# Dilated window attention and a mixer on one core: batch 1's mask moved to VectorE, with a new order of batch 0's channel mix

## The chip, the cores and the metric

The kernel runs on one core of one Trainium2 chip. The core has TensorE (PE in the views, its weight loads PEld), VectorE (DVE), ScalarE (ACT), GpSimd (POOL) and SyncE (SP), which here only issues DMAs. The metric is the device time of one execution in microseconds; less is better. The time given for a kernel is the median of its runs.

## The reference, cut to what matters

```python
B, H, S, D = 8, 8, 576, 64                      # q, k, v: [B, H, S, D], fp32
scores = q @ k.T / sqrt(D)                      # per batch and head
rel = pos[:, None] - pos[None, :]
mask_plain = (rel >= 0) & (rel < 32)            # heads 0 to 3
mask_dil = (rel >= 0) & (rel < 128) & (rel % 4 == 0)   # heads 4 to 7
attn = softmax(where(mask, scores, -1e9))
x = (attn @ v) -> [B, S, 512]                   # heads side by side
h = relu(x.T @ w_tok1) @ w_tok2                 # token mix: 576 -> 256 -> 576
u = x + h.T
out = u + relu(u @ w_ch1) @ w_ch2               # channel mix: 512 -> 1536 -> 512
```

## The kernel before, in words

All products run in fp16 with fp32 sums in PSUM. The eight batches pass one after the other through the same stages; while the channel mix of batch b runs on TensorE, the attention and the token mix of batch b+1 and the preparation of batch b+2 are woven in between. Tokens are taken in two orders: natural for heads 0 to 3 (the plain ones), by residue modulo 4 for heads 4 to 7 (the dilated ones), so that both masks become narrow bands.

**Attention.** q and k are loaded as fp32 in two halves each, cast to fp16 (`cast_qk`, mostly on GpSimd), and turned. In batches 0 and 1 TensorE turns them (`transposes`, L303), in batch 2 too (`bare_steps`, L363), from batch 3 on a DMA does it from SP's queue (`dma_steps`, L348), and GpSimd puts the keys in natural order (`place_steps`, L393, its copies at L396, L399 and L402). Heads come in four pairs hp, two plain and two dilated. `scores_plain` and `scores_dil` (L453, L479) make the score blocks of batches 0 and 1, in two PSUM banks "sc" used in turn, and ScalarE writes their exponentials to `attp`, `attd` and `attt` (the last for the 64 tail queries). Where `veiled` (L428) holds, a product of the identity with `veil`, a block of 0 and -60000, goes into the bank ahead of each score product (L423) and the exponential of the hidden places becomes 0. Elsewhere the exponentials are multiplied by a band of ones and zeros on GpSimd (`mult` at L112). `values` (L592) multiplies by v with a column of ones, into one of three banks "fl"; VectorE takes the reciprocal of the sum (L616) and multiplies (L617, shown as L112) into `xn`.

**Token mix.** `emit_h1` (L619) and `emit_u` (L630) make u; for batch 0 a special `u_half` (L950) does u in ten halves. `emit_uT` (L656) turns u on TensorE in four column blocks cb, which VectorE or, for cb 2, ScalarE copies to SBUF; from batch 2 on a DMA does it.

**Channel mix.** `gen_main` (L747) makes twelve products gp of 128 hidden channels each (`w3`, four column blocks, 512 columns, L768), with a relu on ScalarE or VectorE into `gta`; then the output yp in four row blocks s (0 to 3), each in two halves of 256 columns over the twelve blocks of `w4` (L801). VectorE adds u (L809) and SP stores (L814). An odd batch also does the tails of two batches (L759, L818). gp and yp share three banks "main".

**The order.** Everything is issued in the order in which the program is written, and every engine works its queue in that order. `interleave` (L827) weaves the steps of `gen_main` with a list of steps that each have a due time and a cost: it keeps a clock t, takes the next step of the list if its due time is not after t, and otherwise the next piece of `gen_main`, whose `yield` is its cost. The times are written out by hand per batch (L1017 to L1053); they set an order, nothing waits for them.

**Queues.** SP issues the loads of q, k and v, the turning DMAs and the stores, in program order. The weights go by GpSimd's queue with a cast: `w3` in three parts (L871), `w4` in three thirds of four blocks each (L998 to L1001), between the casts of batch 1 (`casts1`: tails, then q and k by pairs, then four vn, vt, two vd, vx). A `gate` (L866, a one-element copy on GpSimd) keeps SP's loads of batch 2 behind the first block of `w4` (L1006).

Of the kernel before, what the change touches and what calls it, by code (L numbers as in the profile page):

```python
# [20 lines left out]
DM = 512  # L21
# [47 lines left out]
def kernel(  # L69
# [358 lines left out]
    def veiled(b, hp):  # L428
        return b <= 1
# [23 lines left out]
    def scores_plain(b, hp):  # L453
# [20 lines left out]
        if not veils:  # L474
            mult(nc.gpsimd, blocks[:, :, :, 0:BLK], blocks[:, :, :, 0:BLK], band)
            mult(nc.gpsimd, tail_cols(hp), tail_cols(hp), tails_seen[0])
        yield 0.21

    def scores_dil(b, hp):  # L479
        a = attd[hp - 2]  # L480
        diag = a.rearrange("p h (r c) -> p h r c", c=128)
# [11 lines left out]
        if not veils:  # L493
            mult(nc.gpsimd, diag, diag, band[:, :, :, 0:128])
            mult(nc.gpsimd, tail_cols(hp), tail_cols(hp), tails_seen[1])
        yield 0.12

# [158 lines left out]
    def emit_uT(b, cb):  # L656
        odd = b % 2
        p = bank("fl" if b or cb % 2 == 0 else "main", 3, f"tpu_{b}_{cb}", FP16)
# [87 lines left out]

    def gen_main(b):  # L747
# [17 lines left out]
        for mb in range(NMB):  # L765
            p = bank("main", 3, f"gp_{b}_{mb}")
# [4 lines left out]
            relu(nc.vector if (mb % 2 == 1 and mb < 7 if b == 0 else mb % 4 != 3 if b == 1 else mb in (1, 5)) else nc.scalar, gta[:, mb, m0:m0 + 512], p)  # L771
# [5 lines left out]
        for s in ((4, 0, 1, 2, 3) if odd else (0, 1, 2, 3)):  # L777
# [18 lines left out]
            elif s < 4:  # L796
                for half in range(2):
# [10 lines left out]
                    if half:  # L808
                        nc.vector.tensor_tensor(out=blocks4(o32), in0=blocks4(p), in1=u16(b, s), op=ALU.add)  # L809
                        for i in range(2):  # L810
                            d = slice(256 * i, 256 * i + 256)
                            o = out[b, 0:512, d].rearrange("(m r) c -> r m c", r=4)[s] if i else \
                                out[b, 128 * s:128 * s + 128, d]
                            nc.sync.dma_start(out=o, in_=o32[:, d])  # L814
# [12 lines left out]
    def interleave(main, steps):  # L827
# [3 lines left out]
        while main is not None or steps:  # L831
# [4 lines left out]
            else:  # L836
                try:
                    t += next(main)
# [111 lines left out]
    def u_half(s, half):  # L950
        p = bank("main" if half else "fl", 3, f"up_0_{s}_{half}")[:, 0:256]
# [26 lines left out]
    for s in (1, 2):  # L978
        u_half(s, 1)
    for cb in (1, 2, 3):  # L980
        emit_uT(0, cb)
# [14 lines left out]
    for i in (2, 3, 4, 5, 7, 6, 8, 9, 10, 11):  # L996
        casts1[i]()
    for i in range(3):  # L998
        nc.gpsimd.dma_start(
            out=w4a[:, 4 * i:4 * i + 4],  # L1000
            in_=moe_w_ch2[512 * i:512 * i + 512, :].rearrange("(p i) c -> p i c", i=4))  # L1001
    for cast in casts1[12:]:
# [3 lines left out]
    gate(l32[(2, "t")][0:1, 0, 0:1], w4[0][0:1, 0:1])  # L1006
# [77 lines left out]
```

## Time and profile before

| | |
|---|---|
| median of 3 runs | 287.01 us (286.76 to 287.47) |
| the profiled execution | 286.68 us, span of its instructions 284.8 us |
| granted TensorE clock | 0.999 |
| busy, share of the span | TensorE 276.8 us, 97%; GpSimd 163.5, 57%; ScalarE 136.6, 48%; VectorE 130.3, 46% |
| DMA | 52.63 MB, mean 185 GB/s |

How to read it: a time in the views is counted from the start of the span. TensorE's products are pipelined, so a product is listed as longer than the distance to the next one; what one costs is read from start to start, and a busy share of 97% hides breaks shorter than a product's listed length. A row of the timeline merges like instructions that follow each other (x4 is four of them) and gives the idle time ahead of it with what ended it. In the groups, mean ns is the length of one instruction.

### The profile page before, as it was taken

The page shows a single profiled execution, that of the slowest core. Times are in us where ns is not written, and L with a number is a line of the kernel's source. Part 1 is how long each engine was busy: PE and PEld are TensorE (multiplying, and loading weights), DVE is VectorE, ACT ScalarE, POOL GpSimd, SP SyncE. Part 2 cuts the span into 40 slices and gives each one's busy share as a digit, 9 for nine tenths or more (in the row PEclk, how much of TensorE's full clock was granted, in tenths as well). Part 3 has the DMA queues.
Part 4 walks back from the last instruction along what each step waited for, and adds up shares of the span by engine and source line. Part 5 has one row for each costly group of instructions (what it writes and reads, how often), then busy time and mean ns, then how long its engine had stood idle before and what let it go on. Part 6 is the DMA issues. An engine that isn't in the chain of part 4 may idle for free.

```text
span 284.8 us, 7022 instructions
## 1 busy us (share of the span) xinstructions
PE 276.8 (97%) x2850; PEld 211.3 (74%) x2850; DVE 130.3 (46%) x274; ACT 136.6 (48%) x270; POOL 163.5 (57%) x221
## 2 busy tenths in 40 slices
PE   6999999999999999999999999999999999999995
PEld 2796677887775976697776976797767966886594
DVE  7766757356764155415640254426441274421022
ACT  2873575464454714483446625482546534225500
POOL 7980860479964998459961999079943920000000
PEclk9999999999999999999999999999999999999999
DMA  7999999995999999899889997399784210431023
GB/s 220 265 223 237 278 215 200 319 231 139 334 201 181 272 250 240 108 202 344 214 150 226 315 255 151 57 236 297 196 169 82 94 55 2 95 110 37 0 77 111
DMA packets 105695, 52.63 MB, mean 185 GB/s; under 512 B 73888, under 2 KB 104608, under 8 KB 105664
## 3 DMA queue, kind: packets, MB, share of 16 engines
q1 hardware_dynamic: 101424, 47.07, 67.2%
q0 software_dynamic: 2640, 3.94, 7.9%
q10 hardware_dynamic: 1600, 1.18, 1.4%
q8 instruction: 22, 0.36, 0.5%
q14 instruction: 9, 0.07, 0.1%
HBM read 37.07 MB, written 9.44 MB: 163 GB/s over the span
## 4 chain that ended last, share of the span: by engine, by line
PE 90%; DMA 4%; POOL 2%; ACT 1%; DVE 1%; issue 1%; SPq 0%; POOLq 0%; ACTq 0%
PE yp L801 29%; PE gp L768 28%; PE h1p L627 5%; PE up L639 4%; PE gt L759 4%; PE yp L818 3%; PE sc L510 3%; DMA l_k<-in_k_dram 3%; DMA l_q<-in_q_dram 2%; PE av L603 1%; PE av L608 1%; PE h1p L625 1%; PE sc L425 1%; PE sc L423 1%; PE up L650 1%; PE av L601 1%
## 5 line engine op out<-in xcount | busy, mean ns | idle before, releaser
L801 PE MATMUL yp<-w,gt 128*128 128x256 f16 x744 | 85.8, 273 | 0.0
L801 PEld LDWEIGHTS <-gt 128*128 128x128 f16 x744 | 76.1, 106 | 6.4
L106 ACT ACTIVATE gt<-gp 128x512 f16<-128x512 f32 x72 | 43.0, 597 | 75.4 <-PE gp L768 75.1
L768 PE MATMUL gp<-utd,w 128*128 128x512 f16 x144 | 54.7, 380 | 0.0
L768 PE MATMUL gp<-utm,w 128*128 128x512 f16 x144 | 54.6, 379 | 0.0
L768 PEld LDWEIGHTS <-w 128*128 128x128 f16 x384 | 39.0, 114 | 19.9 <-issue 0.5
L809 DVE TENSOR_TENSOR o<-yp,u 128x512 f32<-128x512 f32 x31 | 21.4, 691 | 63.1 <-PE yp L801 54.7
L112 POOL TENSOR_TENSOR attp<-attp,const 128x1280 f16<-128x1280 f16 x12 | 31.4, 2615 | 26.6 <-ACT attp L534 26.5
L112 DVE TENSOR_TENSOR xn<-av,rec 128x320 f16<-128x320 f32 x64 | 31.4, 491 | 2.2
L112 POOL TENSOR_TENSOR attd<-attd,const 128x1024 f16<-128x1024 f16 x12 | 25.4, 2138 | 0.7 <-ACT attd L534 0.7
L768 PE MATMUL gp<-uT,w 128*128 128x512 f16 x96 | 25.6, 379 | 0.0
L108 DVE TENSOR_SCALAR gt<-gp 128x512 f16<-128x512 f32 x24 | 16.5, 687 | 12.0 <-PE gp L768 11.5
L645 DVE TENSOR_TENSOR u<-up,xn 128x512 f16<-128x512 f32 x26 | 17.9, 690 | 6.2 <-PE up L639 6.2
L534 ACT ACTIVATE attp<-sc 128x480 f16<-128x480 f32 (+1 forms) x36 | 16.1, 539 | 7.2 <-PE sc L510 7.2
L102 POOL CAST c_k<-l_k 128x512 f16<-128x512 f32 x29 | 17.8, 622 | 2.0 <-DMA l_k<-in_k_dram 2.0
L102 POOL CAST c_q<-l_q 128x512 f16<-128x512 f32 x27 | 17.4, 650 | 2.5 <-DMA l_q<-in_q_dram 2.5
L616 DVE RECIPROCAL rec<-av 128x5 f32<-128x5 f32 x64 | 12.2, 191 | 13.5 <-PE av L613 13.3
L106 ACT ACTIVATE h<-h1p 128x256 f16<-128x256 f32 x31 | 11.9, 383 | 12.1 <-PE h1p L627 11.7
L399 POOL COPY kt<-kr 128x512 f16<-128x512 f16 x10 | 10.8, 1079 | 10.0 <-DMA kr<-c_k 4.6
L697 ACT COPY utd<-utm 128x512 f16<-128x512 f16 x12 | 12.7, 1130 | 4.0 <-DMA utm<-u 4.0
L102 POOL CAST vv<-l_vn 128x256 f16<-128x256 f32 x32 | 11.8, 412 | 3.8 <-DMA l_vn<-in_v_dram 3.8
L112 POOL TENSOR_TENSOR attt<-attt,const 128x512 f16<-128x512 f16 x12 | 13.9, 1162 | 0.0
(149 smaller groups left out, 465.3 us busy)
## 6 DMA issues: line engine op xcount, KB each, us to landing
out_dram<-o SPq DMA_DIRECT2D x71, 128.0 KB, 3.2
l_q<-in_q_dram SPq DMA_DIRECT2D x15, 512.0 KB, 6.7
l_k<-in_k_dram SPq DMA_DIRECT2D x14, 512.0 KB, 7.0
l_vn<-in_v_dram SPq DMA_DIRECT2D x32, 128.0 KB, 6.5
l_vd<-in_v_dram SPq DMA_DIRECT2D x16, 256.0 KB, 4.6
w<-in_moe_w_ch_dram POOLq DMA_DIRECT2D x6, 512.0 KB, 8.1
lt<-in_q_dram SPq DMA_DIRECT2D x8, 128.0 KB, 5.0
l_vt<-in_v_dram SPq DMA_DIRECT2D x8, 128.0 KB, 4.7
```

The lines of the kernel that those rows point to most:

```text
L102: eng.tensor_copy(out=out, in_=in_)
L106: nc.scalar.activation(out=out, in_=in_, func=AF.Relu)
L108: eng.tensor_scalar_max(out=out, in0=in_, scalar1=0.0)
L112: eng.tensor_tensor(out=out, in0=x, in1=y, op=ALU.mult)
L534: nc.scalar.activation(out=out, in_=in_, func=AF.Exp, scale=0.125)
L616: nc.vector.reciprocal(out=rec[:, :, 0], in_=av[:, :, 64])
L627: nc.tensor.matmul(out=p, lhsT=w[:, s, j], rhs=x[:, s, c], start=False, stop=(s == 3))
L645: nc.vector.tensor_tensor(out=u16(b, s), in0=blocks4(p), in1=blocks4(xn[b][:, s]), op=ALU.add)
L697: nc.scalar.copy(out=natural(uTd[:, cb - 2]), in_=uTm[i][:, cb].rearrange("p r m -> p m r"))
L768: nc.tensor.matmul(out=p, lhsT=w3_block(cb, mb), rhs=uT[(b, cb)][0], start=(i == 0), stop=(i == 3))
L801: nc.tensor.matmul(out=p[:, c], lhsT=gta[:, mb, a0:m0 + 512:4] if half else gta[:, mb, a0:a0 + 128], rhs=w4[mb][:, c], start=(mb == 0), st ...
L809: nc.vector.tensor_tensor(out=blocks4(o32), in0=blocks4(p), in1=u16(b, s), op=ALU.add)
```

## The change

Four edits, with the times of the list moved to suit.

1. **Batch 1 masked by VectorE.** `veiled` holds for batch 0 alone. Batch 1's scores have no product with the veil; a new `mask_pair` multiplies one pair's exponentials and its tails by the band, and the list of batch 0 calls it on VectorE for all four pairs, ahead of the values. Batch 1's cast of q for pair 1 goes from GpSimd to ScalarE.
2. **Batch 0's output by thirds.** Row blocks 0 to 2 of batch 0's output are summed in three rounds, over blocks 0 to 3, 4 to 7 and 8 to 11 of `w4`, with all three banks "main" held. A piece of `gen_main` may now yield ("from", time), which puts the planner's clock forward to 19.2 and 22.4. The first third of `w4` is issued by GpSimd ahead of three of batch 1's v casts, the other two behind them; the gate of batch 2's loads waits for the second third.
3. **Channel product begun amid u.** For the first three gp of batch 0 the column blocks 0 and 1 are multiplied (`gp_first`) between the last u halves and the transposes of column blocks 2 and 3; `gen_main` adds 2 and 3. Two transposes and one u half change their banks for it, and the relus of gp 5 and 6 are on VectorE.
4. **Batch 3's transposes ahead of v.** In batch 1's list the loads of v and the turning DMAs of batch 3 are mixed: four v loads, tails and first k, three v loads, first q and second k, the last v load, second q. GpSimd's placing of keys moves ahead of the last v casts.

```diff
     def veiled(b, hp):
-        return b <= 1
+        return b == 0
...
+    def mask_pair(hp, eng):
+        if hp < 2:
+            w = plain_blocks(hp)[:, :, :, 0:BLK]
+            mult(eng, w, w, band)
+        else:
+            w = attd[hp - 2].rearrange("p h (r c) -> p h r c", c=128)
+            mult(eng, w, w, band[:, :, :, 0:128])
+        mult(eng, tail_cols(hp), tail_cols(hp), tails_seen[hp // 2])
...
+    def gp_first(mb, cb):
+
+        if mb == len(first):
+            first.append(bank("main", 3, f"gp_0_{mb}"))
+        nc.tensor.matmul(out=first[mb], lhsT=w3[0][:, cb, mb:512:4], rhs=uT[(0, cb)][0],
+                         start=(cb == 0), stop=(cb == 3))
...
         for mb in range(NMB):
+            if b == 0 and mb < 3:
+                gp_first(mb, 2)
+                gp_first(mb, 3)
+                relu(nc.vector if mb == 1 else nc.scalar, gta[:, mb, 0:512], first[mb])
+                yield 0.43
+                continue
...
+        if b == 0:
+            ps3 = [bank("main", 3, f"yp_{b}_{s}") for s in range(3)]
+            for i in range(3):
+                if i:
+                    yield ("from", (0.0, 19.2, 22.4)[i])
+                for s, p in enumerate(ps3):
+                    for half in range(2):
+                        c = slice(256 * half, 256 * half + 256)
+                        for mb in range(4 * i, 4 * i + 4):
+                            nc.tensor.matmul(
...
+                        if half or i < 2:
+                            yield 0.43
+                    if i == 2:
...
+                        store(s, o32)
+                        yield 0.43
-        for s in ((4, 0, 1, 2, 3) if odd else (0, 1, 2, 3)):
+        for s in ((4, 0, 1, 2, 3) if odd else (0, 1, 2, 3) if b else (3,)):
...
-                    t += next(main)
+                    d = next(main)
+                    t = max(t, d[1]) if isinstance(d, tuple) else t + d
...
     emit_uT(0, 0)
-    for s in (1, 2):
-        u_half(s, 1)
-    for cb in (1, 2, 3):
-        emit_uT(0, cb)
+    u_half(1, 1)
+    emit_uT(0, 1)
+    gp_first(0, 0)
+    u_half(2, 1)
+    gp_first(1, 0)
+    gp_first(2, 0)
+    for mb in range(3):
+        gp_first(mb, 1)
+    emit_uT(0, 2)
+    emit_uT(0, 3)
...
-    for i in (2, 3, 4, 5, 7, 6, 8, 9, 10, 11):
+    for i in (2, 4, 5, 7, 6, 8):
         casts1[i]()
...
+    load_w4(0)
+    for i in (9, 10, 11):
+        casts1[i]()
+    load_w4(1)
+    load_w4(2)
     for cast in casts1[12:]:
         cast()
 
     new_qk(2)
-    gate(l32[(2, "t")][0:1, 0, 0:1], w4[0][0:1, 0:1])
+    gate(l32[(2, "t")][0:1, 0, 0:1], w4[4][0:1, 0:1])
...
         if b == 0:
+            steps += at(2.9, 0.0, [lambda: cast_qk(1, "q", 1, nc.scalar)])
             steps += score_steps(1, 0, 0, (0.0, 0.7, 1.5),
-                                 ((3.0, 5.2), (4.4, 7.0), (7.2, 9.6), (8.6, 11.4)))
-            va = value_steps(1, 13.4, 0.7)
-            steps += va[:4] + [(p + 0.3, c, f) for p, c, f in va[4:]]
-            steps += mix_steps(1, 18.4, 20.8, 22.8, 31.4, 1.1)
-            steps += at(24.0, 0.3, cast_steps(2))
+                                 ((3.0, 4.9), (4.3, 6.6), (6.9, 9.2), (8.3, 11.0)))
+            steps += at(12.2, 0.0, [lambda: mask_pair(0, nc.vector), lambda: mask_pair(1, nc.vector)])
+            steps += at(13.0, 0.0, [lambda: mask_pair(2, nc.vector)]) + at(13.4, 0.0, [lambda: mask_pair(3, nc.vector)])
+            steps += value_steps(1, 15.0, 0.75)
+            steps += mix_steps(1, 19.5, 22.3, 24.4, 30.0, 1.0)
+            steps += at(23.8, 0.3, cast_steps(2))
...
-            scores2 = score_steps(2, 29.6, 4.4, lag=0.25)
+            scores2 = score_steps(2, 31.4, 4.4, lag=0.25)
...
         elif b == 1:
...
-            steps += at(6.0, 0.0, [lambda: load_v(3)]) + at(20.8, 0.9, load_steps(4))
-            steps += at(11.0, 0.9, dma_steps(3)) + at(16.4, 0.4, place_steps(3))
+            steps += at(20.8, 0.9, load_steps(4))
...
+            steps += at(6.0, 0.0, [lambda: some_v(0, 4)]) + at(8.1, 0.0, [turns[0], turns[2], lambda: some_v(4, 7)])
+            steps += at(10.6, 0.0, [turns[1], turns[4], lambda: some_v(7, 8)]) + at(12.6, 0.0, [turns[3]])
+            steps += at(11.0, 0.3, casts[9:14]) + at(12.5, 0.0, places[0:3])
+            steps += at(13.0, 0.3, casts[14:16]) + at(14.0, 0.0, places[3:]) + at(14.2, 0.0, casts[16:])
```

More of the change, by code (lines that the diff above doesn't have):

```diff
@@ L809, in gen_main @@
                         nc.vector.tensor_tensor(out=blocks4(o32), in0=blocks4(p), in1=u16(b, s), op=ALU.add)
[L810 to L814, printed above, removed]
+                        store(s, o32)
                     yield 0.65
```

38 lines of the change are left out of this document (24 added, 14 removed).

## The prediction

> **What bounds the kernel now.** I read the chain that ended last first, then TensorE's timeline from the end of batch 0's u to the end of batch 1's channel product (20 to 95 us), then GpSimd's, VectorE's and the SP queue's over the same stretch.
>
> ```profile
> PE 90%; DMA 4%; POOL 2%; ACT 1%; DVE 1%; issue 1%; SPq 0%; POOLq 0%; ACTq 0%
> ...
> 79.30 1.73 PE gp L768 x8
> ...
> 95.04 7.97 PE yp L801 x72
> ```
>
> The first line is the chain by engine: TensorE has 90% of it. The two pieces give its pitch: 1.73/8 = 0.216 us for a channel product of 512 columns, 7.97/72 = 0.111 us for an output product of 256. Time therefore goes where TensorE gets less work or fewer breaks; an operation on another engine counts only where TensorE waits for it. The change edits the stage from 26 to 67 us (batch 0's channel mix, with batch 1's attention woven in) and one wait at 89 us. Later batches have the same code.
>
> **Veils taken off TensorE: -2.4 us.** Every score product of batch 1 has an identity product of the same shape ahead of it (L423), whose start to the next start is its price:
>
> ```profile
> 34.95 0.19 PE L423 MATMUL sm<-veil,const 128*128 128x64 f16 x1
> 34.98 0.19 PE L425 MATMUL sm<-qz,kt 128*128 128x64 f16 x1
> ...
> 35.18 0.23 PE L423 MATMUL sc<-veil,const 128*128 128x160 f16 x1
> 35.25 0.23 PE L425 MATMUL sc<-qz,kt 128*128 128x160 f16 x1
> ...
> 37.94 0.22 PE L423 MATMUL sc<-veil,const 128*128 128x128 f16 x1
> 38.00 0.22 PE L425 MATMUL sc<-qz,kt 128*128 128x128 f16 x1
> ```
>
> That is 0.03, 0.07 and 0.055 us. From the code, two plain pairs have 6 products of 160 columns, 2 of 128 and 4 of 64 each; two dilated pairs have 8 of 128 and 4 of 64. So 12 x 0.07 + 20 x 0.055 + 16 x 0.03 = 2.4 us, all of it on TensorE and in the chain.
>
> **Channel product begun amid u: +0.26 us.** Six of batch 0's products (three rows of blocks by two column blocks) are issued before the transposes of column blocks 2 and 3 instead of behind them.
>
> ```profile
> 26.02 0.91 PE L673 MATMUL tpu<-const,u 128*128 128x128 f16 x8
> ...
> 27.38 0.11 PEld L768 LDWEIGHTS <-w 128*128 128x128 f16 x1 [0.28 <-issue]
> 27.71 2.05 PEld L768 LDWEIGHTS <-w 128*128 128x128 f16 x10 [0.22 <-issue]
> ```
> ```profile
> 26.74 0.58 ACT L100 COPY uT<-tpu 128x512 f16<-128x512 f16 x1 [0.38 <-PE tpu L673]
> ...
> 26.97 0.69 DVE L102 COPY uT<-tpu 128x512 f16<-128x512 f16 x1 [0.33 <-PE tpu L673]
> ```
>
> Now the third product waits for ScalarE's copy (to 27.32) and the fourth for VectorE's (to 27.66); the fourth starts at 27.71, so the eighth at 27.71 + 4 x 0.216 = 28.57. After the change the six products fill the breaks around the last u, and the eight transposes come behind them: six products of 0.216 more in front, less the breaks they fill, move the end of the transposes from 26.7 to 27.8. Behind them stands nothing that needs no copy. Reading the trace's distances (last transpose of a block to the end of its copy 0.9 to 1.0 us), the seventh product starts at about 28.5 and the eighth at 28.83. The breaks are moved, not removed: 0.26 us later. Bounds: -0.4 if the copies overlap better, +0.5 if the six products also wait for PSUM banks of u.
>
> **Breaks among the scores: 0, within 0.8.** The pieces up to the first output product:
>
> ```profile
> 42.01 0.19 PE L603 MATMUL av<-vv,attp 128*128 128x65 f16 x1
> ...
> 42.29 0.60 PE L768 MATMUL gp<-uT,w 128*128 128x512 f16 x2
> ...
> 46.51 0.28 PE L608 MATMUL av<-vv,attd 128*128 128x65 f16 x4
> ...
> 46.70 0.27 PE L625 MATMUL h1p<-xn,w1t 128*128 128x256 f16 x1
> ...
> 47.24 0.29 PE L608 MATMUL av<-vv,attd 128*128 128x65 f16 x4
> ...
> 48.83 0.82 PE L801 MATMUL yp<-w,gt 128*128 128x256 f16 x6
> ```
>
> A plain head's value products take 0.28 us, a dilated head's 0.19, one h1 product 0.54. From 28.57 to 48.83 are 20.26 us; less veils (2.4), eight heads (4 x 0.28 + 4 x 0.19 = 1.9) and two h1 products (1.1), which the change moves behind the first output products, 14.9 remain. Work in that is 41 channel products (8.84), 36 transposes (36 x 0.055 = 2.0) and the scores (2.4, as the veils), 13.2 us: 1.7 us are breaks, for casts, for VectorE's copies of keys and for the two score banks that ScalarE has to empty. After the change the scores follow each other in half the time, so the banks turn more slowly beside them; but a half of a channel product stands between more of them. Laying out the new order I find four breaks of 0.1 to 0.6 us, again 1.7. The first output product then starts at 28.83 + 13.2 + 1.7 = 43.7.
>
> **Weight thirds: 0.** GpSimd issues the first third of w4 before three of batch 1's v casts, and one q cast goes to ScalarE.
>
> ```profile
> 29.91 0.77 POOL L871 DMA_DIRECT2D w<-in_moe_w_ch_dram  x1
> ...
> 33.86 1.17 POOL L102 CAST c_k<-l_k 128x512 f16<-128x512 f32 x2 [0.16 <-DMA l_k<-in_k_dram]
> ...
> 38.51 1.61 POOL L999 DMA_DIRECT2D w<-in_moe_w_ch_dram  x3
> 40.10 0.43 POOL L102 CAST vv<-l_vn 128x256 f16<-128x256 f32 x1
> 40.44 0.64 POOL L102 CAST vv<-l_vt 64x512 f16<-64x512 f32 x1
> 41.00 1.20 POOL L102 CAST vv<-l_vd 128x512 f16<-128x512 f32 x2
> 42.29 0.40 POOL L102 CAST vt<-l_vx 128x256 f16<-128x256 f32 x1
> 44.50 0.18 POOL L867 CAST lt<-w 1x1 f32<-1x1 f16 x1 [1.81 <-DMA w<-in_moe_w_ch_dram]
> ```
> ```profile
> DMA to landing us min/median/max: 5.1/7.9/10.6
> ```
>
> The last k cast ends at 35.0, so the third leaves then and lands at 42.9 by the median for w: 0.8 before 43.7. It costs nothing, down to 0.8 later; at the slowest landing, 45.6, TensorE waits 1.9. w3's last part (issued 29.91, so 37.8) is needed by the ninth row of products at about 38.3, 0.5 later. The second and third thirds are wanted only at about 50. What is queued behind: the v casts, wanted by the values at 45, and the gate of batch 2's loads, which now waits for the second third. It opens at 44.50 now and about 1 to 2 us later then. Batch 2's transposes and scores are also put later, by about as much in their places, so I count 0.
>
> **Masks on VectorE, and the values behind them: +0.9 us.** VectorE gets four masks and four tail masks, and queued behind them on VectorE are the reciprocals and products of all eight heads, for whose PSUM banks TensorE waits. The trace shows no product of two SBUF operands on VectorE; the nearest rows:
>
> ```profile
> L112 DVE TENSOR_TENSOR xn<-av,rec 128x320 f16<-128x320 f32 x64 | 31.4, 491 | 2.2
> ...
> L809 DVE TENSOR_TENSOR o<-yp,u 128x512 f32<-128x512 f32 x31 | 21.4, 691 | 63.1 <-PE yp L801 54.7
> ```
> ```profile
> 55.11 0.28 DVE L372 COPY kt<-tp_t 128x256 f16<-128x256 f16 x1
> ...
> 65.23 0.42 DVE L387 COPY kr<-tp_k 128x512 f16<-128x512 f16 x1 [0.22 <-PE tp_k L378]
> ```
> ```profile
> 45.25 0.18 DVE L616 RECIPROCAL rec<-av 128x5 f32<-128x5 f32 x1
> ...
> 45.88 0.18 DVE L616 RECIPROCAL rec<-av 128x5 f32<-128x5 f32 x1
> ```
>
> Products with an fp32 operand grow by (691 - 491)/192 = 1.04 ns an element, dense fp16 copies by 0.14/256 = 0.55 ns. The masks are dense fp16 (1280, 1280, 1024, 1024 elements and four of 256). By the products' line they take 2 x 1.49 + 2 x 1.22 + 4 x 0.42 = 7.1 us, by the copies' line 2 x 0.84 + 2 x 0.70 + 4 x 0.28 = 4.2. I take 4.2, since operands, type and stride are those of the copies, and keep 7.1 for the range. In the layout above the last key transposes of batch 1 start at 39.0 and VectorE's copy of them ends at about 40.4, so the masks end at 44.6; three half-thirds of output (0.44 each) put the first head on TensorE at 45.0 and its reciprocal at 45.5. So the masks are hidden with 0.9 to spare; at 7.1 they would end at 47.5, 2.0 too late, and the whole gain below would be gone. The Trainium skill gives the reason in "VectorE: DVE Perf Modes", section on the perf-mode tier table: a tensor_tensor on 16-bit SBUF operands runs at two elements a cycle, one with fp32 or PSUM at one. By that rule the masks take 4.2 and the sum stays; the two lines above, fp32 against fp16, agree with it, though neither has both operands in SBUF.
>
> Not hidden is what follows. One head takes VectorE 0.63 us (45.25 to 45.88), 0.66 with the plain ones. Five heads and two h1 products now stand together on TensorE with three banks between them. The second h1 product needs the bank of the seventh head: 45.5 + 7 x 0.66 = 50.1. TensorE's own work from 45.0 up to there (eight heads 1.9, three half-thirds 1.3, one h1 0.54) would let it start at 48.7: breaks of 1.5, rounded. In the trace these heads hid under channel products. From 48.83 to the stage's end at 67.44 are 18.6 us; the same count of pieces (96 output products, two h1, u, 56 transposes, batch 2's first scores) leaves about 0.6 of breaks there, mostly before batch 2's transposes, which now come later than their data. So 1.5 - 0.6 = +0.9, between -0.6 (neither) and +1.5 (both).
>
> **Batch 3's transposes ahead of v: -0.6 us.**
>
> ```profile
> 67.44 1.03 PE L768 MATMUL gp<-uT,w 128*128 128x512 f16 x4
> ...
> 88.58 0.38 PE L510 MATMUL sc<-qt,kt 64*128 64x160 f16 x6
> 89.31 0.44 PE L510 MATMUL sc<-qt,kt 64*128 64x160 f16 x8 [0.35 <-POOL kt L399]
> ```
> ```profile
> 83.39 1.28 SPq L351 DMA_TRANSPOSE kr<-c_k  x1
> ```
> ```profile
> 88.19 1.06 POOL L399 COPY kt<-kr 128x512 f16<-128x512 f16 x1
> ```
>
> The keys of batch 3 are turned by a DMA that SP issues at 83.39, behind all eight v loads; GpSimd then places them to 89.25, and TensorE has stood since about 88.8. The change puts tails and first keys ahead of four v loads, so about 5 us sooner. These transposes wait for GpSimd's casts, and behind them on SP now wait those v loads and the second half of q; the v casts come later for it, but batch 3's values are a stage away. The break of 0.5 and the tenth before it go. If TensorE comes to this place 1.2 us sooner (2.4 - 0.26 - 0.9), the unmoved order would have cost as much more, so the move also keeps what the rest wins.
>
> **Sum.** -2.4 + 0.26 + 0 + 0 + 0.9 - 0.6 = -1.8 us. The profiled execution took 286.68 us (span 284.8, 1.9 around it); so 284.9 against it. The median of the three runs is 287.01, 0.33 above it: 285.2 us.
>
> **The rivals.**
>
> *Masks meet GpSimd's casts.* Between 40 and 45 us GpSimd casts v: 0.43 + 0.64 + 1.20 + 0.40 = 2.7 us. If each operation that starts first holds up the other, up to 2.7 us falls on the masks; they end at 47.3, 1.8 later than the first reciprocal, and all banks with it. Of the gain of 1.8 nothing is left: 287.0. Against it: casts come as v lands, in pieces, and half of them may fall on GpSimd instead. The Trainium skill states this lock in "SBUF — State Buffer", section on who interferes with whom: a VectorE operation with two SBUF inputs and a GpSimd one that reads SBUF exclude each other. No operation of that kind is in the trace of before, so it neither agrees nor differs. Chance 0.13.
>
> *VectorE becomes the bound (slower).* The masks run by the products' line, 7.1 us, and half of the casts (1.35) fall on them: end at 40.4 + 8.45 = 48.9, 3.4 past the first reciprocal. Against the gain of 1.8 that is +1.6: 288.6. It decides once the masks end later than 45.5 + 1.8 = 47.3. For it: the only products in the trace run at that line. Against: both have an fp32 operand in them. Chance 0.11.
>
> *Loads take the win.* Either w4's first third lands as late as the slowest w (1.9 us of TensorE's time), or the gate opens 2 us later and batch 2's masks on GpSimd come late for its values: a gain of 0 to 0.4, about 286.8. This is the case of a change that doesn't bring its weight sooner. For it: DMA engines are full in this stretch. Chance 0.09.
>
> *No new breaks.* TensorE runs on through the values (-1.5) and the lead-in costs nothing (-0.3): 283.4. Chance 0.15.
>
> **How the numbers follow.** Forecast 285.2, chance 0.52; its own range by the bounds of breaks and lead-in is 284.1 to 286.4. About 0.3% (0.9 us) is what a measurement of this kernel can tell from no change: below 286.1 is faster, above 287.9 slower. Faster: forecast and the last rival and a little of the others, 0.66. Same: 0.22. Slower: 0.12. The range leaves out the slower rival and what lies beyond the last one: 283.2 to 287.2.
>
> **What would show it.** Right: no L423 after 20 us; mask rows of about 0.84 and 0.70 us on VectorE; TensorE's breaks between the first head and the second h1 product about 1.5 us, released by VectorE; batch 1's first channel product at about 66.2 instead of 67.44; no wait for L399 at batch 3's first scores. Wrong: mask rows over 1.2 us or starting only when GpSimd's casts end; TensorE standing for w before the first output product; values of batch 2 waiting for GpSimd's masks; a break among the scores over 1 us.

## The result and the profile after

The changed kernel takes 292.00 us (median of 6 runs, 289.70 to 293.01) against 286.88 us for the kernel before in the same session (6 runs, 286.17 to 287.56): 1.0167 times as long, interval 1.0137 to 1.0197. It is slower by 1.7%, where I forecast 285.2. The profiled execution took 292.29 us, its span 290.4. The six executions differ in the granted clock: one at 1.000 took 289.70 us, two at 0.993 and 0.994 took 291.71 and 290.76, three at 0.987 and 0.988 took 292.29 to 293.01; the profile is one of these three.

The page of the changed kernel, the line of 40 slices with the granted clock and the chain by engine:

```profile
PEclk9999999797999999999999999999999999999999
...
PE 83%; DMA 6%; SPq 3%; issue 2%; DVE 2%; POOL 2%; ACT 1%; POOLq 0%; ACTq 0%
```

TensorE had 90% of the chain before, DMA 4%, "issue" 1% and SP's queue nothing; now TensorE has 83%, and DMA, SP's queue and "issue" together 11%. And two slices, near 50 and near 70 us, show a lower granted clock, which the kernel before did not have there. Next, TensorE's timeline of the changed kernel from 30 us on, with only the rows that show a wait, then the first product of batch 1's channel mix and batch 3's first scores:

```profile
34.29 0.38 PE L425 MATMUL sc<-qz,kt 128*128 128x160 f16 x3 [0.45 <-DVE kt L314]
...
36.56 0.38 PE L425 MATMUL sc<-qz,kt 128*128 128x160 f16 x3 [0.36 <-DVE kt L314]
...
41.29 0.38 PE L425 MATMUL sc<-qz,kt 128*128 128x128 f16 x4 [0.40 <-ACT attd L484]
...
49.27 0.19 PE L613 MATMUL av<-vt,attt 128*128 128x65 f16 x1 [1.26 <-POOL vt L102]
...
50.40 0.27 PE L627 MATMUL h1p<-xn,w1t 128*128 128x256 f16 x1 [0.54 <-DVE rec L618]
...
51.58 0.37 PE L627 MATMUL h1p<-xn,w1t 128*128 128x256 f16 x1 [0.17 <-ACT h L106]
...
65.06 0.80 PE L512 MATMUL sc<-qt,kt 64*128 64x160 f16 x12 [0.28 <-ACT uT L100]
...
66.28 0.23 PE L512 MATMUL sc<-qt,kt 64*128 64x128 f16 x2 [0.42 <-DVE uT L102]
...
68.06 0.59 PE L675 MATMUL tpu<-const,u 128*128 128x128 f16 x4 [1.38 <-ACT attt L536]
...
73.78 1.03 PE L785 MATMUL gp<-uT,w 128*128 128x512 f16 x4
...
94.91 0.65 PE L512 MATMUL sc<-qt,kt 64*128 64x160 f16 x14
```

The stage ends at 73.78 where it ended at 67.44: 6.3 us lost between 26 and 74 us. From there to the end of the span are 216.6 us, against 217.4 before: 0.7 comes back, at the row at 94.91, batch 3's first scores, which no longer wait for GpSimd. The idle time in brackets is counted from a product's listed end; from start to start, less what the product before it costs, the breaks are 0.15 to 0.2 longer (1.42 at 49.27, 1.54 at 68.06).

Why TensorE waits at 49.27 is read from the queues. SP's issues of the last v load and of batch 2's first load in the kernel before:

```profile
34.75 1.50 SPq L207 DMA_DIRECT2D l_vx<-in_v_dram  x1
44.70 0.61 SPq L196 DMA_DIRECT2D lt<-in_q_dram  x1
```

The same two in the changed kernel:

```profile
34.49 1.60 SPq L207 DMA_DIRECT2D l_vx<-in_v_dram  x1
49.37 0.61 SPq L196 DMA_DIRECT2D lt<-in_q_dram  x1
```

And GpSimd's timeline in the changed kernel:

```profile
34.66 0.54 POOL L1048 DMA_DIRECT2D w<-in_moe_w_ch_dram  x1
...
38.23 1.07 POOL L1048 DMA_DIRECT2D w<-in_moe_w_ch_dram  x2
...
42.65 1.06 POOL L102 CAST vv<-l_vd 128x512 f16<-128x512 f32 x1 [1.84 <-DMA l_vd<-in_v_dram]
48.82 0.40 POOL L102 CAST vt<-l_vx 128x256 f16<-128x256 f32 x1 [5.11 <-DMA l_vx<-in_v_dram]
49.16 0.18 POOL L909 CAST lt<-w 1x1 f32<-1x1 f16 x1
```

The last v load of batch 1 (l_vx) leaves SP a quarter of a microsecond sooner than before, and yet lands at 48.8; before, its cast began at 42.29. That is 14.3 us from issue to landing instead of 7.5, with all three thirds of the output weight under way beside it. GpSimd stands 5.1 us for it, and the gate, which is behind that cast in GpSimd's queue, opens at 49.16 instead of 44.50. So batch 2's loads are 4.7 us late as well (whether that costs anything is the second experiment's question).

The clock, by windows of 2 us (busy time of PE, PEld, DVE, ACT and POOL, then granted clock, DMA share, GB/s):

```profile
48.00:50.00 2.00, 0.60 (x15) 0.46 (x13) 1.05 (x4) 0.00 (x0) 0.52 (x2) 1.00 0.06 13
50.00:52.00 2.00, 1.43 (x14) 1.07 (x15) 1.90 (x7) 0.38 (x1) 0.00 (x0) 0.76 0.41 93
52.00:54.00 2.00, 2.00 (x11) 1.40 (x10) 0.17 (x1) 0.38 (x1) 0.61 (x1) 0.50 0.88 242
54.00:56.00 2.00, 2.00 (x18) 1.73 (x17) 0.00 (x0) 0.38 (x1) 0.61 (x1) 0.89 1.10 367
...
68.00:70.00 2.00, 1.94 (x15) 1.69 (x15) 1.21 (x2) 1.86 (x5) 0.98 (x1) 0.52 0.67 134
70.00:72.00 2.00, 2.00 (x17) 1.66 (x16) 0.01 (x1) 0.58 (x1) 2.00 (x2) 0.62 0.89 292
```

The DMA engines are nearly idle from 48 to 50 us (share 0.06): everything waits for the gate. And behind each group of breaks TensorE gets half its clock for a while. The clock missing from 50 to 56 us is 2 x (0.24 + 0.50 + 0.11) = 1.7 us, that from 68 to 72 is 2 x (0.48 + 0.38) = 1.7 us: two stretches of 3.4 us at 0.50. A row listed as busy 2.00 there does half the work: twelve output products take 2.2 us from 52.60 on, where they took 1.3 from 44.01 on.

Last, the masks on VectorE, four of eight rows:

```profile
40.53 0.95 DVE L112 TENSOR_TENSOR attp<-attp,const 128x1280 f16<-128x1280 f16 x1
...
42.55 0.68 DVE L112 TENSOR_TENSOR attd<-attd,const 128x1024 f16<-128x1024 f16 x1
43.15 0.70 DVE L112 TENSOR_TENSOR attt<-attt,const 128x256 f16<-128x256 f16 x1
...
44.38 0.28 DVE L112 TENSOR_TENSOR attt<-attt,const 128x256 f16<-128x256 f16 x1
```

They end at 44.66 and are hidden. A meeting with GpSimd shows: its cast at 42.65 begins just behind the mask at 42.55 and takes 1.06 instead of 0.63 us; the mask at 43.15 begins while that cast runs and takes 0.70 instead of 0.28. By the Trainium skill ("SBUF — State Buffer", on who interferes with whom) the later of two such operations is blocked until the earlier one is done; the trace agrees, at 0.4 us each time.

### The profile page after: what moved, and what is told of

Read it like the earlier page. It is cut to its first block, busy times and chain, and to the rows that moved or that the text cites. A ratio compares the mean times of both kernels' runs of the same rounds, so it can differ in the third digit from the quotient of the medians.

```text
span 290.4 us, 6934 instructions
## 1 busy us (share of the span) xinstructions
PE 277.5 (96%) x2802; PEld 210.9 (73%) x2802; DVE 134.7 (46%) x283; ACT 136.1 (47%) x270; POOL 163.4 (56%) x220
## 4 chain that ended last, share of the span: by engine, by line
PE 83%; DMA 6%; SPq 3%; issue 2%; DVE 2%; POOL 2%; ACT 1%; POOLq 0%; ACTq 0%
PE yp L846 26%; PE gp L785 25%; PE h1p L629 5%; PE up L641 4%; PE gt L770 4%; PE yp L859 4%; DMA l_vd<-in_v_dram 3%; PE sc L512 3%; SPq L207 2%; PE yp L811 2%; DMA w1p<-in_moe_w_tok_dram 2%; DMA l_q<-in_q_dram 1%; PE h1p L627 1%; PE av L610 1%; PE av L605 1%
## 5 line engine op out<-in xcount | busy, mean ns | idle before, releaser
L846 PE MATMUL yp<-w,gt 128*128 128x256 f16 x672 | 77.3, 275 | 0.0
L106 ACT ACTIVATE gt<-gp 128x512 f16<-128x512 f32 x71 | 42.4, 597 | 71.6 <-PE gp L785 70.3
L846 PEld LDWEIGHTS <-gt 128*128 128x128 f16 x672 | 69.5, 107 | 5.9
L785 PEld LDWEIGHTS <-w 128*128 128x128 f16 x372 | 38.0, 114 | 19.4
L854 DVE TENSOR_TENSOR o<-yp,u 128x512 f32<-128x512 f32 x28 | 19.4, 692 | 59.6 <-PE yp L846 55.8
L112 DVE TENSOR_TENSOR xn<-av,rec 128x320 f16<-128x320 f32 x64 | 31.5, 492 | 2.2
L108 DVE TENSOR_SCALAR gt<-gp 128x512 f16<-128x512 f32 x25 | 17.2, 688 | 12.2 <-PE gp L785 10.7
L785 PE MATMUL gp<-uT,w 128*128 128x512 f16 x84 | 22.0, 380 | 0.0
L102 POOL CAST c_q<-l_q 128x512 f16<-128x512 f32 x26 | 16.8, 653 | 3.1 <-DMA l_q<-in_q_dram 3.1
L656 DVE TENSOR_TENSOR u16t<-up,xn 64x512 f16<-64x512 f32 x7 | 4.8, 688 | 20.7 <-PE up L652 20.7
```

The lines of the kernel that those rows point to most:

```text
L102: eng.tensor_copy(out=out, in_=in_)
L106: nc.scalar.activation(out=out, in_=in_, func=AF.Relu)
L108: eng.tensor_scalar_max(out=out, in0=in_, scalar1=0.0)
L112: eng.tensor_tensor(out=out, in0=x, in1=y, op=ALU.mult)
L785: nc.tensor.matmul(out=p, lhsT=w3_block(cb, mb), rhs=uT[(b, cb)][0], start=(i == 0), stop=(i == 3))
L846: nc.tensor.matmul(out=p[:, c], lhsT=gta[:, mb, a0:m0 + 512:4] if half else gta[:, mb, a0:a0 + 128], rhs=w4[mb][:, c], start=(mb == 0), st ...
```

## The experiments

The theory after the result: the weight, issued sooner, takes the DMA engines from the last v load; that makes TensorE wait and opens the gate late (the wait is shown below, a cost of the late gate is not); batch 2's transposes and scores then meet the transposes of batch 1's u in the three banks "fl"; and each group of breaks brings half clock. The rivals: the gate's new condition is to blame, or the new order of products has lost its cover whatever the loads do. All ratios are against the kernel before, run beside each on the same chip: 286.61 us for the first four kernels, 286.73 for edits 1, 3 and 4 alone and the mended kernel, 286.53 for the loads alone and the last two.

**The gate on the first third (changed kernel).**

```diff
-    gate(l32[(2, "t")][0:1, 0, 0:1], w4[4][0:1, 0:1])
+    gate(l32[(2, "t")][0:1, 0, 0:1], w4[0][0:1, 0:1])
```

> The changed kernel, with the gate of batch 2's loads back on the first third of w4. Theory A (the gate's one-element copy stands in GpSimd's queue behind the last v cast, whose load landed at 48.8 us, so the tile that it names decides nothing): the gate opens at 49.2 as in the changed kernel, time unchanged within 0.3%. Rival B (waiting for the second third makes batch 2 late): the gate opens about 44.5 and the time falls by 1 to 2 us.

Measured: 291.34 us, 1.0128 [1.0080, 1.0177], which can't be told from the changed kernel's 1.0167. GpSimd's gate copy still starts at 49.53, because it stands behind the cast of l_vx, which waits to 49.19. The condition of the gate is not what holds it; its place in the queue is.

**The second and third third of the weight behind the v casts (and the gate on the first).**

```diff
-    load_w4(1)
-    load_w4(2)
     for cast in casts1[12:]:
         cast()
+    load_w4(1)
+    load_w4(2)
```

> The changed kernel, with the second and third thirds of w4 issued behind all v casts of batch 1, and the gate on the first third. Theory A (those thirds crowd out the last two v loads): the last v load lands near 43.5 instead of 48.8, TensorE's break of 1.4 us before the fifth head is gone, the half clock from 51 to 54.5 us (1.7 us) too, the gate opens near 44.5 and batch 2's data come some 3 to 4 us sooner: 2.5 to 4 us less than the changed kernel (288 to 289.5). Rival (the first third alone crowds the v load out, or the later thirds come too late for the second round of the output): break of over 1 us stays, time within 0.5% of the changed kernel.

Measured: 290.13 us, 1.0105 [1.0072, 1.0137]. GpSimd in this kernel:

```profile
43.82 0.46 POOL L102 CAST vt<-l_vx 128x256 f16<-128x256 f32 x1
44.22 1.12 POOL L1048 DMA_DIRECT2D w<-in_moe_w_ch_dram  x2
45.33 0.18 POOL L909 CAST lt<-w 1x1 f32<-1x1 f16 x1
```

The cast no longer waits, so the load was in by 43.8, five microseconds sooner (8.9 us after its issue, against 14.3), and the gate opens at 45.33. The break for vt is gone; those that are left before the second h1 product are 0.53, 0.53 and 0.45 us, all released by VectorE and ScalarE. So the two late thirds did starve the v load, and repairing that brings back 1.6 of the 5.1 us, less than the 2.5 to 4 expected: three of the four executions still ran at 0.993 or 0.994.

The breaks at batch 2 are the same to 0.01 us, with 1.54 at the worst. But the open gate did not bring batch 2's data sooner, as the two thirds now stand beside these loads. GpSimd's first cast of batch 2 in the changed kernel:

```profile
53.38 0.61 POOL L102 CAST c_t<-lt 128x512 f16<-128x512 f32 x1 [4.04 <-DMA lt<-in_k_dram]
```

And with the thirds behind the v casts:

```profile
54.90 0.62 POOL L102 CAST c_t<-lt 128x512 f16<-128x512 f32 x1 [9.39 <-PE up L652]
```

The first is the load of the k tails, which takes 3.2 us from issue to landing in the changed kernel and 8.6 in this one. Its data come 1.5 us later and the breaks are the same: so the late gate of the changed kernel is not what makes them.

**The last two transposes of batch 1's u in the other banks (changed kernel).**

```diff
-        p = bank("fl", 3, f"tpu_{b}_{cb}", FP16) if b or cb % 2 == 0 else bank("sc", 2, f"tpu_{b}_{cb}", FP16)
+        p = bank("main", 3, f"tpu_{b}_{cb}", FP16) if b == 1 and cb % 2 else \
+            bank("fl", 3, f"tpu_{b}_{cb}", FP16) if b or cb % 2 == 0 else bank("sc", 2, f"tpu_{b}_{cb}", FP16)
```

> The changed kernel, with the last two transposes of batch 1's u in banks main instead of fl. Theory C (they stand right behind batch 2's first scores, which hold the three fl banks until ScalarE has done four small exponentials): the break of 1.5 us before them falls under 0.4, and the half clock from 68 to 71.5 (1.7 us) goes with it: 1.5 to 3 us less than the changed kernel, 289 to 290.5. Rival (the wait is for the late data of batch 2 and only moves): under 0.8 us less.

Measured: 290.33 us (288.44 to 291.38), 1.0103 [1.0071, 1.0135]. TensorE's rows that answer, these transposes, the output products behind them and the next wait:

```profile
64.79 0.40 PE L675 MATMUL tpu<-const,u 128*128 128x128 f16 x4
...
65.67 0.82 PE L846 MATMUL yp<-w,gt 128*128 128x256 f16 x6
...
68.39 0.38 PE L378 MATMUL tp_k<-const,c_k 128*128 128x128 f16 x4 [0.58 <-DVE kt L388]
```

The break of 1.54 before the transposes is 0.09 now: the banks were its cause. But the output products behind them now wait 0.31, and a new break of 0.75 comes at 68.39 for VectorE's copy of keys, so only 0.4 us of it is gained. The stage ends at 69.9 in this execution, which is one of full clock. This kernel also prices the half clock: its eight executions fall into three at a granted clock of 1.000 (288.44 to 288.71 us) and five at 0.994 (290.24 to 291.38). The same instructions, with medians 1.9 us apart. A stretch of 1.7 us lost in 290 is 0.006 of the clock, so 0.994 is one such stretch and the 0.987 of the changed kernel's profile is two.

**Idle products in the two worst breaks (changed kernel).** Six products of 512 columns without use at due time 17.5 and six at 31.5; they add work to the kernel and take nothing out.

```diff
+    def fill(tag, bufs, n):
+        p = bank(tag, bufs, f"fill_{tag}")
+        for _ in range(n):
+            nc.tensor.matmul(out=p, lhsT=idle[:, 0:128], rhs=idle, start=True, stop=True)
...
+            steps += at(17.5, 0.0, [lambda: fill("sc", 2, 6)]) + at(31.5, 0.0, [lambda: fill("main", 3, 6)])
```

> The changed kernel, with six idle products of 512 columns (1.3 us) on TensorE ahead of the fifth head of batch 1 and six ahead of the last two transposes of u, each in the place of a wait of about 1.5 us. They compute nothing that is used. Theory D (the granted clock falls to a half for some 3.4 us after such a wait, which costs 1.7 us each time): clock 1.00 through both stretches, 2 to 3.4 us less than the changed kernel, 288.6 to 290. Rival (the half clock has another cause): clock as in the changed kernel, time the same or up to 0.5 us more.

Measured: 289.55 us (289.29 to 290.29), 1.0093 [1.0064, 1.0123]; against the 291.34 of the gate's kernel beside it, which has the breaks open. The windows:

```profile
50.00:52.00 2.00, 1.32 (x15) 1.07 (x16) 1.90 (x7) 0.38 (x1) 0.00 (x0) 1.00 0.53 116
52.00:54.00 2.00, 2.00 (x21) 1.84 (x20) 0.14 (x1) 0.39 (x1) 0.56 (x1) 1.00 0.94 260
...
68.00:70.00 2.00, 2.00 (x29) 1.92 (x27) 1.00 (x4) 1.47 (x4) 2.00 (x1) 1.00 0.63 149
```

The late v load, the late gate and the other breaks are still there; only the two waits are filled and the half clock is gone, in all four executions, and with it 1.8 us. The time is that of the changed kernel's one execution at full clock, 289.70. So the half clock follows from TensorE's standing and is a cost of its own.

**Edit 1 alone on the kernel before, without its q cast: masks on VectorE, values later.**

```diff
-        return b <= 1
+        return b == 0
...
+            steps += at(12.2, 0.0, [lambda: mask_pair(0, nc.vector), lambda: mask_pair(1, nc.vector)])
+            steps += at(13.0, 0.0, [lambda: mask_pair(2, nc.vector)]) + at(13.4, 0.0, [lambda: mask_pair(3, nc.vector)])
+            steps += value_steps(1, 16.0, 0.7)
+            steps += mix_steps(1, 20.6, 22.6, 24.2, 31.4, 1.1)
```

> The kernel before with the masks of batch 1 on VectorE and its values later, and nothing else of the change: the weight of the output product is issued and landed as before. Theory (TensorE saves the veils' 2.4 us, but arrives at the first output product at about 43.4 us, where the weight lands by parts at 44.4, 46.8 and 50.2 in the kernel before): TensorE waits 2 to 4 us in all for the weight instead, so the time is 286.5 to 288.5. Rival (the order of products fills the gap, and nothing else is short): the whole 2.4 us less, 284.5. The rival is also what my forecast would have said of this part alone.

Measured: 292.65 us, 1.0197 [1.0167, 1.0228]: slower, and by more than I expected. TensorE's waits:

```profile
44.90 0.61 PE L804 MATMUL yp<-w,gt 128*128 128x256 f16 x4 [1.26 <-DMA w<-in_moe_w_ch_dram]
...
47.35 1.01 PE L804 MATMUL yp<-w,gt 128*128 128x256 f16 x4 [1.84 <-DMA w<-in_moe_w_ch_dram]
...
50.52 1.01 PE L804 MATMUL yp<-w,gt 128*128 128x256 f16 x4 [2.16 <-DMA w<-in_moe_w_ch_dram]
```

From start to start, less the product before it, 1.43, 2.01 and 2.37: 5.8 us, with half clock from 46.58 to 53.41. Without the veils, and with values and h1 moved behind, TensorE is at the output product at 43.5 us, where it came at 48.8 before, and the weight lands when it always did. My theory had the right wait and missed its size, as I had left out that all twelve blocks are needed by the first half, and the clock.

**The loads of edit 2 alone on the kernel before.** Nothing else: veils, whole output products and all times of the list as before, but for the one q cast on ScalarE.

```diff
-    for i in (2, 3, 4, 5, 7, 6, 8, 9, 10, 11):
+    for i in (2, 4, 5, 7, 6, 8):
         casts1[i]()
...
+    load_w4(0)
+    for i in (9, 10, 11):
+        casts1[i]()
+    load_w4(1)
+    load_w4(2)
...
-    gate(l32[(2, "t")][0:1, 0, 0:1], w4[0][0:1, 0:1])
+    gate(l32[(2, "t")][0:1, 0, 0:1], w4[4][0:1, 0:1])
```

> The kernel before with only the loads of the change: the weight's first third issued ahead of three casts, the second and third right behind them, the gate hung on the second third, one q cast on ScalarE; the veils, the whole output products and all else as before. Theory (the late v load and the late gate cost by themselves): the last v load of batch 1 lands at about 48 us instead of 42.2, its first reader on TensorE (45 to 46.6 us before) waits 2 to 3 us for it, and batch 2's first transposes wait 1 to 2 us at 57 us; with the half clock that follows, 289.5 to 292. Rival (the loads were harmless, and the loss of the change belongs to the products that now come without cover): 286.5 to 287.5.

Measured: 293.93 us, 1.0245 [1.0218, 1.0272], the slowest of all. GpSimd's row for vt in this kernel:

```profile
49.32 0.40 POOL L102 CAST vt<-l_vx 128x256 f16<-128x256 f32 x1 [4.27 <-DMA l_vx<-in_v_dram]
```

TensorE's row behind it:

```profile
49.77 0.21 PE L611 MATMUL av<-vt,attt 128*128 128x65 f16 x1 [5.39 <-POOL vt L102]
```

That is one wait of 5.6 us from start to start, less the product before it. The windows of this kernel at that place:

```profile
46.00:48.00 2.00, 0.00 (x0) 0.00 (x0) 0.00 (x0) 0.00 (x0) 0.00 (x0) 0.77 0.49 95
48.00:50.00 2.00, 0.23 (x3) 0.21 (x3) 0.00 (x0) 0.00 (x0) 0.52 (x2) 0.50 0.05 10
50.00:52.00 2.00, 2.00 (x12) 0.91 (x10) 1.37 (x4) 0.60 (x1) 0.00 (x0) 0.50 0.28 65
52.00:54.00 2.00, 2.00 (x14) 1.20 (x13) 0.67 (x2) 0.60 (x1) 0.00 (x0) 0.53 0.82 191
```

The place and the cause are the theory's; the wait is twice what I gave it, since it is the fifth head that reads vt and it was ready at 44.2. The other wait of the theory did not come: the gate opens at 49.66, and yet TensorE has no break over 0.1 us from 49.8 to 64 us, so the late gate costs nothing here either. The rival is out: the loads harm by themselves, with every product of before in its place. It also shows why the whole change is less bad than this part of it: there the values come later, and TensorE reaches vt at 47.9.

**Edit 3 alone (channel product amid u), edit 4 alone (batch 3's transposes ahead of v).** Their diffs are edits 3 (without the two relus) and 4 of the change, put on the kernel before.

> The kernel before with the channel product begun amid u and nothing else. Theory: the eighth channel product starts 0.23 to 0.26 us later than before and that stays: 286.9 to 287.2, within 0.3% of before. Rival (the new banks of the transposes let later work run closer): 286.2 or less.

> The kernel before with batch 3's transposes ahead of v and nothing else. Theory: the break of 0.61 us before batch 3's first scores goes, and no other comes: 286.1 to 286.4. Rival (the v casts that come later for it open a break of the same size): 286.7 to 287.2.

Measured: edit 3 286.98 us, 1.0011 [0.9989, 1.0034]; edit 4 286.20 us, 0.9987 [0.9967, 1.0006]. Both are where the theory put them, and neither can be told from no change. In the second the break before batch 3's first scores is gone from the trace.

**The changed kernel mended.** The loads as in the second experiment, and all four transposes of batch 1's u in banks "main".

```diff
-        p = bank("fl", 3, f"tpu_{b}_{cb}", FP16) if b or cb % 2 == 0 else bank("sc", 2, f"tpu_{b}_{cb}", FP16)
+        p = bank("main", 3, f"tpu_{b}_{cb}", FP16) if b == 1 else \
+            bank("fl", 3, f"tpu_{b}_{cb}", FP16) if b or cb % 2 == 0 else bank("sc", 2, f"tpu_{b}_{cb}", FP16)
```

> The changed kernel with three things mended at once: the second and third thirds of the weight issued behind batch 1's v casts, the gate hung on the first third, and all four transposes of batch 1's u in banks of the scores' own kind. Theory (the loss is the late v load, the late gate, the full banks, and the half clock that the breaks bring): no break over 1 us between 40 and 70 us, no slice of granted clock under 0.8 there, the first channel product of batch 1 at 67 to 68.5 us, and the time 286 to 288. Rival (something of the changed kernel that I have not seen costs 3 us or more by itself): over 289 with the breaks gone.

Measured: 287.93 us (12 runs, 287.58 to 288.83), 1.0042 [1.0028, 1.0056], every execution at a granted clock of 0.998 or more. Of the 5.1 us lost, 3.9 are back, so the causes named are three quarters of it; the two repairs come to 3.0 one by one (1.6 and 1.4). The stage ends at 69.36, a microsecond later than the theory had it. The breaks that are left are all of 0.75 us or less: 1.9 us among batch 1's scores, 1.5 among its values, 2.4 at batch 2's transposes and scores.

**The mended kernel with more room between its steps, twice.** The first puts the gate ahead of the second and third third of the weight, batch 1's scores at their old due times and batch 2's transposes further apart; the second also spreads the heads and puts the last pair's masks later.

```diff
-                                 ((3.0, 4.9), (4.3, 6.6), (6.9, 9.2), (8.3, 11.0)))
+                                 ((3.0, 5.2), (4.4, 7.0), (7.2, 9.6), (8.6, 11.4)))
...
-            steps += [(t, 0.25, f) for t, f in zip((27.2, 28.4, 29.0, 29.6, 30.2, 33.6, 34.0, 34.4, 34.8), bare)]
+            steps += [(t, 0.25, f) for t, f in zip((26.8, 27.8, 28.6, 29.6, 30.4, 33.6, 34.4, 35.2, 36.0), bare)]
```
```diff
-            steps += value_steps(1, 15.0, 0.75)
+            steps += value_steps(1, 15.0, 0.85)
```

> The mended kernel with the gate ahead of the second and third thirds of the weight, the scores of batch 1 at the due times of the kernel before (0.3 to 0.4 us later each), and batch 2's transposes further apart. Theory (what is left of the loss are 1.9 us of breaks among scores, 1.5 among values and 2.2 at batch 2's transposes, each of them a matter of spacing): under 1 us of breaks among the scores, under 1.5 at batch 2's transposes, and 286 to 287. Rival (VectorE and ScalarE set these breaks, so that they move and don't go): 287.5 to 288.5.

> As spaced, and batch 1's heads 0.1 us further apart, with the last pair's masks put behind the second head. Theory: the three breaks of 0.5 us among values go to two or fewer, 0.5 us less than spaced, 285.5 to 286.5. Rival (VectorE's 0.7 us for one head is the bound there): the same as spaced.

Measured: 287.07 us, 1.0014 [0.9996, 1.0031], and 287.41 us, 1.0029 [1.0010, 1.0048]. The room at batch 2's transposes helped (2.4 us of breaks became 1.3). Among the scores it did not: 1.9 became 0.18 + 1.10 + 0.38 = 1.7, the longest now for VectorE's copy of keys. Among the values 1.5 became 1.4. There the rivals hold: VectorE and ScalarE set these breaks, and the room only moves them. Neither time is clearly the theory's (286 to 287, and 285.5 to 286.5).

No version is faster than the kernel before by more than the measurement tells; edit 4 alone is the lowest.

## Why the prediction was wrong

**What held.** The veils went from TensorE (2.4 us). The eighth channel product starts at 28.80, forecast 28.83. The breaks among the scores are 0.61, 0.53, 0.18 and 0.57, 1.9 us in all, forecast 1.7, four of them as laid out. The first output product starts at 44.01, forecast 43.7; the first third of the weight is in, and TensorE does not wait for it. The masks take 4.1 us and end at 44.66, forecast 4.2 and 44.6; neither the rival of the casts nor that of VectorE came about. Batch 3's break went. And where v was in time (the second experiment), the breaks among the values were 0.53 + 0.53 + 0.45 = 1.5 us, as forecast.

**The step that failed: "Weight thirds: 0".** I asked when each third would land and what stood behind it in GpSimd's queue, and found the v casts and the gate. I did not ask what stood beside it on the DMA engines: the last v loads, which SP issues from 32 to 36 us and which were still under way. I wrote "DMA engines are full in this stretch" in the rival of the loads, and used it only against the weight, not against v. And I let the gate wait for the weight, while it also waits for the v cast ahead of it. Shown by two edits in opposite directions: the loads alone cost 7.4 us on the kernel before (the v load lands after 14.7 us instead of 7.5), and taking the two late thirds back brings the v load of the changed kernel from 48.8 to under 43.8. Where I had 0, the break of 1.42 us at 49.27 puts the second h1 product 1.2 us behind its forecast, and it helps to bring the half clock. The late gate cost nothing that these runs show.

Why v loses so much shows in the queues' packets of the changed kernel from 42 to 48 us (packets, MB, share of 16 engines' time):

```profile
q0 software_dynamic: 289, 1.04, 87.2%
q1 hardware_dynamic: 220, 0.05, 6.5%
```

The first is GpSimd's queue with the weight, the second SP's with the v loads. A packet of the weight takes 0.872 x 6 x 16 / 289 = 0.29 us in the mean, one of v 0.065 x 6 x 16 / 220 = 0.028. The Trainium skill says in "DMA: Bandwidth & Descriptors", section on queues, rings and completion order, that a DMA engine takes turns between its queues by packet. The trace fits that: the two queues pass 289 and 220 packets, not far from one for one, and so the weight has nine tenths of the time. In the kernel before v is nearly through when the weight comes: from 38 to 42 us SP's queue passes 911 packets and the weight 76. The landing times agree as well: the last of the weight passes at about 48.3, l_vx comes in at 48.8, and 13 GB/s are left in the window from 48 to 50 us.

**The second step that failed: the breaks "mostly before batch 2's transposes, which now come later than their data".** They did come later than their data. But at their new due times they and batch 2's scores stand against the transposes of u with no output halves between, and three banks for all: 0.27 + 0.17 + 0.44 + 0.16 + 0.58 + 1.54 = 3.2 us of breaks where I had none. I counted pieces and their data, and not the banks, which I had counted for the values. That the banks did it is shown for the 1.54 (0.09 with other banks) and argued for the 0.44 and 0.58, which are released by the copies of uT that empty such banks.

**What was in no step: the clock.** I priced a break at its length. Here breaks of 1.42 and 0.70 us within 2.6 us, or of 0.58 and 1.54 within 2.4, were followed by 3.4 us at half clock, 1.7 us each time: the price of such breaks is nearly twice their length. The Trainium skill ("TensorE: Matmul & The Clock Gate", part 1) has windows of about 3.4 us that run freely, with half rate after an idle one. The length agrees with both stretches here (3.4 us each), and so do their starts, 51.03 and 68.09, which are five such lengths apart. The condition does not: TensorE was not idle for a whole window, only for some 2 us in it. Laid on this grid, the windows of the changed kernel are:

```profile
47.62:51.03 3.41, 1.61 (x36) 1.27 (x32) 2.39 (x9) 0.00 (x0) 0.52 (x2) 1.00 0.10 21
51.03:54.44 3.41, 3.24 (x21) 2.27 (x20) 1.11 (x3) 0.77 (x2) 0.61 (x1) 0.50 0.86 236
64.68:68.09 3.41, 1.33 (x27) 0.97 (x26) 1.55 (x3) 1.62 (x6) 0.80 (x2) 1.00 0.49 163
68.09:71.51 3.42, 3.42 (x24) 2.87 (x24) 1.22 (x2) 2.25 (x5) 2.49 (x1) 0.50 0.75 194
```

With TensorE listed as busy for 1.61 and 1.33 us, the next window runs at half. In twelve of the thirteen traces, those that record when the clock changes, all eight windows with 1.61 us or less were followed by half clock, and no window with 1.77 or more was. The same breaks of 0.44, 0.16, 0.58 and 1.54 us, which fill one window here, are divided by a window's end at 65.11 in the trace of the second experiment:

```profile
61.70:65.11 3.41, 2.02 (x39) 1.59 (x37) 1.69 (x3) 1.27 (x4) 3.07 (x8) 1.00 1.03 278
```

That one ran on at full clock, while the three other executions of the same kernel did not. By these figures, whether breaks cost the 1.7 us depends on where the windows happen to lie, and the same instructions run at 1.000 in some executions and at 0.994 in others.

**The sum.** The stage's end was forecast at 66.2 and came at 73.8, 7.6 later: 0.3 at the first output product, 1.2 more up to the second h1 product (51.58 instead of 50.1, less those 0.3), 3.2 of breaks at batch 2's transposes and scores, 3.1 of half clock (of the first stretch's 1.7, 0.3 lie before the second h1 product and are in the 1.2), less 0.2 that I cannot place. The rest of the span came as forecast.

**And the gain itself.** With all that mended the kernel is still 1.2 us slower than before, where the sum has 1.8 faster. The veils' 2.4 us were gained among the scores and lost again behind them, as TensorE came sooner to places where data or banks were not ready: the kernel before has 0.6 us of breaks from 43 us to the end of the stage, the mended one 4.2 (0.3 at the first output product, 1.5 among the values, 2.4 at batch 2), and only those of the values I had forecast. For edit 1 alone the wait behind is shown (5.8 us for the weight); that the mended kernel's 2.4 at batch 2 could not be avoided is not shown, and with more room they became 1.3 and the time 287.07. Edit 1 alone and the loads alone each cost more (5.9 and 7.4 us) than the change with both (5.1), as each takes away some of the other's wait.

## What to carry to other kernels

Before a transfer is issued sooner, list what else is in flight in the same microseconds on every queue, and whose reader has the least room; a transfer with packets of 0.29 us doubled the time of one with packets of 0.028 us that was issued before it. Follow a gate back through all that stands ahead of it in its engine's queue, not only to its own condition. On TensorE, where breaks come to 2 us or more within 3.4 us, add the 1.7 us that the half clock cost here, as it comes in some executions of a kernel and not in others; and count work taken off it as a gain only where the next data and the next bank are there sooner too.

## What was not expected of the hardware

The half clock behind breaks that are far from an idle window: a stretch of 3.4 us at 0.50, 1.7 us lost, behind each window of 3.4 us in which TensorE was listed as busy for 1.61 us or less, and so in some executions of the same kernel and not in others (288.4 to 288.7 us against 290.2 to 291.4). And a load issued before the weight that took 14.3 us instead of 7.5 beside it.
